# Products of the identity at the start of an attention and gated MLP kernel, and its last whole-tile store in two halves

## The chip, the cores and the metric

The kernel runs on one core of one Trainium2 chip. The metric is the device time of one execution in microseconds (us). Every time of the profile comes from one profiled execution, counted from its span's start.

## The reference

Batch 8, 16 query heads that share 4 key and value heads, 384 positions, head width 64. The attention's output, with its heads laid side by side, is the 1024-wide input x of a gated MLP:

```python
attn = softmax((q @ k.T) / sqrt(64))          # k, v repeated for 4 query heads each
x = (attn @ v).transpose(0, 2, 1, 3).reshape(8, 384, 1024)
h = maximum(x @ w_in, 0)                      # 1024 -> 1024
u, v = h[..., :512], h[..., 512:]
v_n = (v - mean(v)) / sqrt(var(v) + 1e-6)     # over the 512
v_s = einsum('ts,bsd->btd', w_spatial, v_n) + b_spatial[None, :, None]
out = (u * v_s) @ w_out                       # 512 -> 1024, float32
```

## The kernel before, in words

**Work of one batch.** Queries and keys are loaded as float32 (L199, L212), cast to 16 bits (L223, L234; the cast itself is in the helper `copy`, L322) and transposed, in batches 0 and 1 by TensorE against the identity (L328, L343, with a copy out of PSUM after it, L337, L352), from batch 2 on by transposing DMAs on SyncE's queue (L304, L313). A score step (`S`, L361) is two products of 64 rows that run side by side; its exponential (`E`, L375) is one ScalarE instruction of 128x1024. There are 18 of both in a batch, and two PSUM buffers for scores, so a score step waits for the exponential two before it. A value step (`X`, L386) is 12 products on 32-column parts, either of the values or of ones (the sums). The sums become reciprocals on ScalarE (`rl`, `re`; once on VectorE, `rv`), and `xm` (L418) multiplies into x transposed.

The MLP has the V products (`V` or, as halves of 64 rows, `v_part`), relu (`ru`), statistics (`bs`), `rs` and normalization (`nm`), the products with w_spatial (`SP`, `gs`) and their bias (`sa`), the U products (`U`, `gu`) and the gate (`gt`), and the output products (`O`, `go`) with their copies (`oc`) and stores (`st`, L560).

**Paired products.** A step `G` (L676) issues two chains of 64-row products that run side by side: the low rows of one tile with the high rows of another, in a first phase, and the rest in a second. The second phase must not start before the first has ended, and this is carried by a mark (`mk`, L689): a one-element memset on VectorE or GpSimd, which waits for the first phase in that engine's queue and on which the second phase waits. The kinds `w12`, `w24` and `w10` pair V products of one batch with output products of another.

**Weights.** w_in comes in 8 loads on GpSimd's queue (`lwi`, L245; part 1 is for V, part 0 for U). w_spatial comes in one load (`lws`), three GpSimd casts (`cws`, L269) and TensorE transposes (`Tw`), w_out in four loads (`lwo`, L252) that share two buffers, each cast in two halves (`cwo`). The transposing DMAs of batch 2 wait for all loads of w_in's part 0 (`behind_w_in`, L299).

**Order.** Three lists set the order: `FIRST` for batches 0 to 2 and what they prepare, `STEADY` for each of batches 3 to 6, and `LAST`. Each step names its kind, the batch (relative to the one run) and its arguments; the last letter of some names the engine (`p` GpSimd, `v` VectorE, `s` ScalarE). `run` (L727) goes through a list, and each engine, and each engine's DMA queue, executes its own steps strictly in the list's order. PSUM for all but the scores is four banks in a queue: `bank` takes the one free for longest, and the last reader gives it back, so the list also decides which reader a product waits for. A step `W` (L698) exists, but no list has it.

**The end.** The last output products are `O,0,2`, `O,0,3` and `lo,0,5` (L564). `lo` makes two pieces of 256 columns, one copied by VectorE and stored by SyncE, one copied and stored by ScalarE. `st,0,1` stores the tile of `O,0,2` and `O,0,3`, 128x1024.

Of the kernel before, what the change touches and what calls it, by code (L numbers as in the profile page):

```python
# [14 lines left out]
PE, POOL, SP = mybir.EngineType.PE, mybir.EngineType.Pool, mybir.EngineType.SP  # L15
# [3 lines left out]
SPLIT = 0  # L19

FIRST = """
lk,0,0,2 lq,0,0,0,1,0,1,s cq,0,0,0,1,1,0,1,s lq,0,1,0,1 cq,0,0,0,1,0,0,1,v lk,0,2,4 ck,0,0,0,3,p
Tq,0,0,0,0,1 Tk,0,0,0,3 tq,0,0,0,0,1,s lq,0,0,1,3 lq,0,1,1,3 tk,0,0,0,3,v lk,1 lv,0 ck,0,1,0,3,p S,0
S,0 lv,1 Tk,0,1,0,3 cq,0,1,0,1,0,0,1,p cq,0,1,0,1,1,0,1,p lq,1,0 lws,0 lq,1,1 Tq,0,1,0,0,1 lbi,0
lq,2,0 lq,2,1 lk,2 lwi,0,1,0 lwi,0,1,1 tk,0,1,0,3,v cq,0,0,1,3,1,0,1,p lwi,0,1,3 lwi,0,1,2
tq,0,1,0,0,1,v cq,0,0,1,3,0,0,1,v E,0 S,0 S,0 ck,1,0,0,3,p ck,1,1,0,3,p cv,0,p Tq,0,0,2,0,1 E,0 E,0
S,0 Tq,0,0,1,0,1 E,0 S,0 E,0 cq,0,1,1,3,1,0,1,v tq,0,0,1,0,1,v S,0 cq,0,1,1,3,0,0,1,v E,0
Tq,0,1,2,0,1 Tq,0,1,1,0,1 S,0 Tk,1,0,0,3 tq,0,1,1,0,1,v E,0 S,0 tk,1,0,0,3,v tq,0,0,2,0,1,v
tq,0,1,2,0,1,v E,0 X,0,0,2 rv,0,0 S,0 E,0 X,0,0,0 S,0 E,0 E,0 S,0 X,0,0,1 E,0 S,0 X,0,1,2 E,0
X,0,1,0 rl,0,1 cq,1,0,0,1,0,0,1,p lwi,0,0,2 cq,1,0,1,3,1,0,1,p xm,0,0,1 xm,0,0,0 S,0 S,0 cws,0,0  # L30
cws,0,1 lwi,0,0,3 cws,0,2 lwi,0,0,0 cq,1,1,0,1,0,0,1,p X,0,1,1 V,0,0,0,4 E,0 lwi,0,0,1 cv,1,p E,0
re,0,1 S,0 E,0 S,0 cq,1,1,1,3,0,0,1,p cq,1,0,0,1,1,0,1,s V,0,0,4,8 Tk,1,1,0,3 xm,0,1,1 xm,0,1,0
cq,2,0,0,3,1,0,1,p cq,2,0,0,3,0,0,1,p S,0 E,0 tk,1,1,0,3,v cq,1,0,1,3,0,0,1,v ru,0,0,v Tq,1,0,0,0,1
V,0,1,0,4 E,0 X,0,2,2 tq,1,0,0,0,1,s bs,0,0 rl,0,2 ck,2,1,0,3,p ck,2,0,0,3,p cq,2,1,0,3,0,0,1,p
X,0,2,1 S,0 S,0 cq,1,1,0,1,1,0,1,v re,0,2 E,0 X,0,2,0 cq,2,1,0,3,1,0,1,p Tq,1,1,0,0,1 xm,0,2,1
tq,1,1,0,0,1,v V,0,1,4,8 xm,0,2,0 S,0 S,0 ru,0,1,v E,0 Tq,1,0,1,0,1 Tw,0,2,3 Tq,1,0,2,0,1 V,0,2,0,4
cq,1,1,1,3,1,0,1,v S,0 S,0 E,0 tq,1,0,1,0,1,v tw,0,2,3 Tq,1,1,1,0,1 E,0 E,0 E,0 Tw,0,0,2 V,0,2,4,8
tq,1,1,1,0,1,v tq,1,0,2,0,1,v bs,0,1 tw,0,0,2 ru,0,2,s bs,0,2 X,1,0,2 rl,1,0 S,0 S,0 X,1,0,0 X,1,0,1
Tq,1,1,2,0,1 re,1,0 xm,1,0,0 S,0 E,0 xm,1,0,1 rs,0 E,0 nm,0,0 lwo,0,1 dq,2,0 nm,0,1 tq,1,1,2,0,1,v
nm,0,2 lwo,0,0 dk,2 dq,2,1 lwo,0,2 lwo,0,3 V,1,0,0,4 lv,2 V,1,0,4,8 E,0 S,0 G,0,gs,2,0,0,1 S,0  # L40
ru,1,0,v mk,0,gs,2,v G,0,gs,0,0,0,1 E,0 G,0,gs,2,1,0,1 S,0 mk,0,gs,0,v sa,0,2 G,0,gs,0,1,0,1 E,0 S,0
E,0 sa,0,3 sa,0,1 X,1,1,2 sa,0,0 E,0 rl,1,1 X,1,1,1 X,1,1,0 S,0 lq,3,1 lk,3 lq,3,0 re,1,1 E,0
G,0,gu,2,0,0 xm,1,1,1 xm,1,1,0 G,0,gu,2,0,1 S,0 S,0 G,0,gu,0,0,0 E,0 G,0,gu,0,0,1 S,0 mk,0,gu,2,v
cwo,0,0,0,v G,0,gu,2,1,0 cwo,0,1,0,p cwo,0,0,1,p mk,0,gu,0,p cwo,0,1,1,p S,0 G,0,gu,0,1,0 S,0
G,0,gu,0,1,1 E,0 gt,0,1 S,0 cwo,0,2,0,p E,0 G,0,gu,2,1,1 gt,0,2 gt,0,3 bs,1,0 gt,0,0 cwo,0,3,0,v E,0
cwo,0,2,1,p S,0 X,1,2,2 X,1,2,1 E,0 cwo,0,3,1,p S,0 S,0 V,1,1,0,4 E,0 V,1,1,4,8 E,0 rl,1,2 S,0
G,0,go,0,0,0 G,0,go,0,0,1 S,0 E,0 E,0 re,1,2 xm,1,2,1 mk,0,go,0,v E,0 G,0,go,0,1,0 E,0 S,0
G,0,go,0,1,1 S,0 cv,2,v ru,1,1,v oc,0,1,v oc,0,0,v cq,3,0,0,3,0,0,1,p cq,3,1,0,3,0,0,1,p E,0
cq,3,1,0,3,1,0,1,p cq,3,0,0,3,1,0,1,p X,1,2,0 xm,1,2,0 X,2,0,2 X,2,0,0 rl,2,0 E,0 S,0 E,0 re,2,0
G,1,w12,2,0,0 G,1,w12,2,0,1 S,0 S,0 bs,1,1 E,0 ck,3,0,0,3,v ck,3,1,0,3,v mk,1,w12,2,v G,1,w12,2,1,0  # L50
G,1,w12,2,1,1 E,0 S,0 S,0 oc,0,2,v ru,1,2,s oc,0,3,v xm,2,0,0 X,2,1,2 E,0 X,2,0,1 X,2,1,1 X,2,1,0
rl,2,1 bs,1,2 xm,2,0,1 re,2,1 S,0 xm,2,1,1 G,2,w24,0,0,0 G,2,w24,0,0,1 rs,1 S,0 E,0 S,0 E,0 E,0 lv,3
xm,2,1,0 mk,2,w24,0,v dk,3 dq,3,0 dq,3,1 nm,1,2 nm,1,0 nm,1,1 G,2,w24,0,1,0 oc,0,4,v G,2,w24,0,1,1
S,0 G,1,gs,0,0,0,1 E,0 ru,2,0,s oc,0,5,v mk,1,gs,0,v S,0 G,1,gs,0,1,0,1 E,0 G,1,gs,2,0,0,1 sa,1,1
mk,1,gs,2,v S,0 G,1,gs,2,1,0,1 sa,1,0 sa,1,2 sa,1,3 S,0 G,1,gu,0,0,0 G,1,gu,0,0,1 G,1,gu,2,0,0 S,0
mk,1,gu,0,v S,0 G,1,gu,2,0,1 G,1,gu,0,1,0 cv,3,p mk,1,gu,2,p S,0 G,1,gu,0,1,1 G,1,gu,2,1,0 E,0 E,0
E,0 S,0 G,1,gu,2,1,1 E,0 E,0 gt,1,0 gt,1,1 gt,1,3 gt,1,2 S,0 E,0 X,2,2,2 X,2,2,0 E,0 rl,2,2
G,2,w10,1,0,0 E,0 re,2,2 G,2,w10,1,0,1 S,0 S,0 E,0 mk,2,w10,1,v bs,2,0 xm,2,2,0 G,2,w10,1,1,0
G,2,w10,1,1,1 S,0 X,2,2,1 E,0 oc,1,1,s lk,4 st,0,0 lq,4,0 st,0,2 lq,4,1 ru,2,1,v xm,2,2,1 oc,1,0,v
st,0,1 E,0 bs,2,1 st,1,0 lv,4  # L60
"""

STEADY = """
X,0,0,2 cq,1,0,0,3,1,0,1,p cq,1,1,0,3,0,0,1,p cq,1,1,0,3,1,0,1,v X,0,0,0 rl,0,0 S,0 G,-1,w12,2,0,0
G,-1,w12,2,0,1 cq,1,0,0,3,0,0,1,p ck,1,1,0,3,p dq,1,1 re,0,0 E,0 ck,1,0,0,3,s S,0 mk,-1,w12,2,v dk,1
dq,1,0 S,0 G,-1,w12,2,1,0 G,-1,w12,2,1,1 E,0 xm,0,0,0 oc,-2,2,v X,0,1,2 E,0 ru,-1,2,s rl,0,1
oc,-2,3,s re,0,1 X,0,0,1 X,0,1,0 bs,-1,2 xm,0,0,1 X,0,1,1 S,0 xm,0,1,0 G,0,w24,0,0,0 G,0,w24,0,0,1
rs,-1 nm,-1,1 xm,0,1,1 mk,0,w24,0,v nm,-1,0 nm,-1,2 S,0 E,0 S,0 G,0,w24,0,1,0 oc,-2,4,v
G,0,w24,0,1,1 E,0 E,0 S,0 G,-1,gs,0,0,0,1 S,0 ru,0,0,s mk,-1,gs,0,p oc,-2,5,v E,0 G,-1,gs,2,0,0,1
bs,0,0 mk,-1,gs,2,v G,-1,gs,0,1,0,1 E,0 sa,-1,1 G,-1,gs,2,1,0,1 S,0 sa,-1,2 sa,-1,3 sa,-1,0 X,0,2,2  # L70
rl,0,2 X,0,2,0 X,0,2,1 S,0 G,-1,gu,0,0,0 G,-1,gu,0,0,1 S,0 re,0,2 E,0 E,0 xm,0,2,0 xm,0,2,1 E,0
G,-1,gu,2,0,0 G,-1,gu,2,0,1 S,0 mk,-1,gu,0,p E,0 G,-1,gu,0,1,0 G,-1,gu,0,1,1 S,0 E,0 mk,-1,gu,2,p
cv,1,p G,-1,gu,2,1,0 G,-1,gu,2,1,1 S,0 S,0 gt,-1,0 gt,-1,1 gt,-1,3 gt,-1,2 G,0,w10,1,0,0
G,0,w10,1,0,1 E,0 S,0 E,0 mk,0,w10,1,v S,0 G,0,w10,1,1,0 G,0,w10,1,1,1 oc,-1,0,v oc,-1,1,v ru,0,1,v
lq,2,0 lv,2 lk,2 S,0 lq,2,1 st,-2,2 st,-2,1 E,0 E,0 E,0 bs,0,1 st,-1,0
"""

LAST = """
S,0 X,0,0,2 E,0 G,-1,w12,2,0,0 G,-1,w12,2,0,1 S,0 mk,-1,w12,2,v S,0 E,0 rl,0,0 re,0,0 G,-1,w12,2,1,0
G,-1,w12,2,1,1 S,0 X,0,1,2 oc,-2,2,v X,0,0,1 oc,-2,3,v rl,0,1 re,0,1 E,0 ru,-1,2,v X,0,1,1 X,0,0,0  # L80
xm,0,0,1 xm,0,1,1 X,0,1,0 xm,0,0,0 S,0 G,0,w24,0,0,0 G,0,w24,0,0,1 E,0 mk,0,w24,0,v E,0 S,0 S,0 E,0
bs,-1,2 xm,0,1,0 G,0,w24,0,1,0 G,0,w24,0,1,1 E,0 oc,-2,4,v ru,0,0,s X,0,2,2 rl,0,2 re,0,2 rs,-1
oc,-2,5,s X,0,2,0 X,0,2,1 xm,0,2,0 xm,0,2,1 nm,-1,0 V,0,1,0,4 V,0,1,4,8 V,0,2,0,4 nm,-1,1 nm,-1,2
U,-1,1 V,0,2,4,8 ru,0,1,s SP,-1,0 SP,-1,1 bs,0,0 ru,0,2,v sa,-1,0 sa,-1,1 bs,0,2 gt,-1,1 bs,0,1
U,-1,0 SP,-1,2 SP,-1,3 rs,0 nm,0,1 sa,-1,2 sa,-1,3 nm,0,0 nm,0,2 gt,-1,0 U,0,0,1 U,-1,2 gt,-1,2
U,-1,3 SP,0,2 gt,-1,3 sa,0,2 SP,0,3 O,-1,4 U,0,2 SP,0,0 sa,0,3 sa,0,0 O,-1,2 O,-1,0 oc,-1,4,v gt,0,2
O,-1,1 oc,-1,0,s oc,-1,1,s O,-1,5 O,-1,3 SP,0,1 oc,-1,5,v oc,-1,2,v sa,0,1 U,0,1 U,0,3 gt,0,0 gt,0,1
gt,0,3 oc,-1,3,s st,-2,2 O,0,0,0,3 st,-2,1 st,-1,2 O,0,4 O,0,1,0,3 oc,0,4,s O,0,0,3,4 O,0,1,3,4
st,-1,1 st,-1,0 oc,0,1,v oc,0,0,s O,0,2 O,0,3 oc,0,2,s oc,0,3,s st,0,2,0,512 st,0,0 lo,0,5 st,0,1
"""  # L90


# [681 lines left out]
```

## Time and profile before

| | us |
|---|---|
| median of 7 runs (249.01 to 251.03) | 250.18 |
| the profiled execution | 249.8 |
| its span | 248.0 |
| TensorE busy, 2505 products | 237.1 |
| ScalarE busy, of it 140.3 in 144 exponentials | 187.4 |
| VectorE busy | 147.1 |
| GpSimd busy | 41.9 |
| DMA read, written | 25.95 MB, 12.58 MB |

A busy TensorE is counted from each product's start to its modelled end, so busy products overlap; the chain of waits, which follows the last instruction back to what released it, shows each product by the time it added. PE is TensorE, PEld its weight loads, DVE VectorE, ACT ScalarE, POOL GpSimd and SP SyncE; a q behind a name is that engine's queue. L366 is line 366 of the code.

### The profile page before, as it was taken

To read this page: it belongs to the slowest core of one execution; us is meant where nothing else is said; L and a number is where in the kernel's file an instruction comes from. 1 tells how busy PE (TensorE), PEld (TensorE's weight loads), DVE (VectorE), ACT (ScalarE), POOL (GpSimd) and SP (SyncE) were. 2 spreads that over 40 slices of the span, in tenths; PEclk is the share of its full clock that TensorE was granted. 3 is DMA by queue.
4 is the path that set the end of the run, shared out by engine and by line. 5 is a ranking of instruction groups with operands and counts; after the bars stand their busy time and mean duration, and the time that the engine had idled before them with its cause. 6 is when DMAs were issued, how large, how long until landed. Compare 5 with 4: busy or idle time off the path is not lost.

```text
span 248.0 us, 5946 instructions
## 1 busy us (share of the span) xinstructions
PE 237.1 (96%) x2505; PEld 112.7 (45%) x2505; DVE 147.1 (59%) x293; ACT 187.4 (76%) x242; POOL 41.9 (17%) x81
## 2 busy tenths in 40 slices
PE   1899999999999999999999999999999999999992
PEld 1334445544445444554455534554445544455451
DVE  0475867358763476835675377835676355678440
ACT  3899999998997797879987897879988777700222
POOL 1813824231401300020200130020300100000000
PEclk9999999999999999999999999999999999999998
DMA  8999999997699159229960689319844020030075
GB/s 177 288 230 347 222 244 282 181 303 225 83 266 340 47 166 179 94 60 355 202 185 3 196 310 178 116 48 281 256 86 172 3 85 3 27 146 0 0 292 216
DMA packets 57610, 42.71 MB, mean 172 GB/s; under 512 B 26864, under 2 KB 53872, under 8 KB 57584
## 3 DMA queue, kind: packets, MB, share of 16 engines
q1 hardware_dynamic: 54224, 39.85, 58.0%
q0 software_dynamic: 2176, 2.10, 5.5%
q10 hardware_dynamic: 1184, 0.39, 0.6%
q8 instruction: 19, 0.31, 0.5%
q14 instruction: 7, 0.06, 0.1%
HBM read 25.95 MB, written 12.58 MB: 155 GB/s over the span
## 4 chain that ended last, share of the span: by engine, by line
PE 90%; DMA 5%; ACT 1%; DVE 1%; issue 1%; SPq 0%; POOL 0%; DVEq 0%; POOLq 0%
PE X L393 20%; PE sc L366 14%; PE po L638 12%; PE pu L611 12%; PE pv L598 11%; PE pv L436 5%; DMA q<-in_q_dram 5%; PE psp L624 5%; PE po L543 4%; PE pu L508 4%; PE pq L347 2%; PE psp L482 2%; ACT aT L379 1%; PE sc_u L508 1%; DVE q L326 0%
## 5 line engine op out<-in xcount | busy, mean ns | idle before, releaser
L379 ACT ACTIVATE aT<-sc 128x1024 f16<-128x1024 f32 x144 | 140.3, 1022 | 20.9 <-PE sc L366 20.4
L638 PE MATMUL po<-w_out,gT 64*128 64x512 f16 x288 | 66.4, 376 | 0.1
L598 PE MATMUL pv<-w_in,xt 64*128 64x512 f16 x272 | 64.2, 376 | 0.0
L366 PE MATMUL sc<-qT,kT 64*128 64x512 f16 x288 | 51.9, 391 | 0.7 <-DVE kT L326 0.5
L422 DVE TENSOR_TENSOR xt<-X,rec 128x512 f16<-128x512 f32 x48 | 31.8, 683 | 12.3 <-ACT rec L410 5.4
L393 PE MATMUL X<-aT,v 128*32 128x512 f16 x576 | 36.3, 379 | 0.0
L611 PE MATMUL pu<-xt,w_in 64*128 64x384 f16 x384 | 35.5, 322 | 0.0
L638 PEld LDWEIGHTS <-gT 64*128 64x128 f16 x288 | 25.6, 94 | 17.0 <-DVE mark_v L692 4.2
L326 DVE COPY osb<-po 128x512 f32<-128x512 f32 x34 | 23.3, 690 | 16.6 <-PE po L638 11.0
L598 PEld LDWEIGHTS <-xt 64*128 64x128 f16 x272 | 25.2, 94 | 14.7 <-issue 0.8
L520 DVE SCALAR_TENSOR_TENSOR gT<-pu,v_s 128x384 f16<-128x384 f32 x31 | 16.0, 551 | 24.2 <-PE pu L611 23.2
L326 POOL CAST q<-q 128x768 f16<-128x768 f32 (+2 forms) x27 | 19.6, 747 | 46.3 <-DMA q<-in_q_dram 36.6
L366 PEld LDWEIGHTS <-kT 64*128 64x128 f16 x288 | 14.9, 94 | 25.4 <-issue 14.3
L611 PEld LDWEIGHTS <-w_in 64*128 64x128 f16 x384 | 18.7, 94 | 13.5
L393 PEld LDWEIGHTS <-v 128*32 128x32 f16 x576 | 16.1, 96 | 14.9 <-issue 2.4
L494 DVE TENSOR_TENSOR v_s<-psp,bias_b 128x384 f32<-128x384 f32 x32 | 20.1, 681 | 4.0 <-PE psp L624 2.6
L457 DVE BATCH_NORM_STATS2 stats<-v_r 128x6 f32<-128x512 f32 x24 | 16.6, 691 | 7.9 <-ACT v_r L449 3.2
L393 PE MATMUL X<-aT,ones 128*32 128x512 f16 x288 | 20.2, 382 | 0.2
L404 ACT ACTIVATE rec<-X 128x512 f32<-128x512 f32 x23 | 13.8, 601 | 7.7 <-PE X L393 7.5
L324 ACT ACTIVATE osb<-po 128x512 f32<-128x512 f32 x13 | 7.7, 594 | 14.7 <-PE po L543 14.7
L694 POOL MEMSET mark_p<- 1x1 f32 x14 | 1.2, 88 | 86.7 <-PE pu L611 43.8
L410 ACT ACTIVATE rec<-rec 128x512 f32<-128x512 f32 x23 | 14.5, 631 | 0.5
(55 smaller groups left out, 187.5 us busy)
## 6 DMA issues: line engine op xcount, KB each, us to landing
out_dram<-osb SPq DMA_DIRECT2D x23, 512.0 KB, 5.0
q<-in_q_dram SPq DMA_DIRECT2D x14, 768.0 KB, 8.0
v<-in_v_dram SPq DMA_DIRECT2D x8, 384.0 KB, 4.5
k<-in_k_dram SPq DMA_DIRECT2D x7, 384.0 KB, 4.4
w_in<-in_moe_w_in_dram POOLq DMA_DIRECT2D x8, 256.0 KB, 7.0
w<-in_moe_w_out_dram SPq DMA_DIRECT2D x4, 512.0 KB, 5.5
q<-in_q_dram SPq DMA_DIRECT2D x2, 512.0 KB, 6.6
ws<-in_moe_w_spatial_dram SPq DMA_DIRECT2D x1, 576.0 KB, 9.5
```

Source lines behind the costliest of these rows:

```text
L326: engine.tensor_copy(dst, src)
L366: nc.tensor.matmul(sc[:, half, 0 : 512 // js], kT[b][lo:hi, gp, t, :], qT[b, gp][lo:hi, qt, j0::js], start=True, stop=True,)
L379: nc.scalar.activation(aT[b, qt][:, gp, t].rearrange("p h (j q) -> p h j q", j=G)[:, :, j0::js], held["sc", b, u, j0][:, :, 0 : 512 // js] ...
L393: nc.tensor.matmul(dst[32 * g : 32 * (g + 1), :], v16[:, g, t, 32 * part : 32 * (part + 1)] if part < 2 else ones32, a[:, g // 2, t, g % 2 ...
L410: nc.scalar.activation(r, r, AF.Exp, scale=-1.0)
L422: nc.vector.tensor_tensor(xt[:, jj, :, qt * P : (qt + 1) * P], held["X", b, qt, jj].rearrange("p (j q) -> p j q", j=G), held["rec", b, qt] ...
L457: nc.vector.bn_stats(s6, held["v_r", b, st])
L494: nc.vector.tensor_tensor(held["v_s", b][:, m, :].rearrange("p (t s) -> p t s", t=NST), held["psp", b, m][:, 0:S].rearrange("p (t s) -> p ...
L520: nc.vector.scalar_tensor_tensor(held["gT", b][:, mu, :], held["pu", b, mu][:, 0:S], 0.0, held["v_s", b][:, mu, :], op0=ALU.max, op1=ALU.mult,
L598: yield lambda kc=kc: nc.tensor.matmul(held["pv", b, st], xT[b][rows, kc, st * P : (st + 1) * P], w_in16[rows, kc, DH:DFF], start=(first a ...
L611: yield lambda kc=kc: nc.tensor.matmul(held["pu", b, mu][:, 0:S], w_in16[rows, kc, mu * P : (mu + 1) * P], xT[b][rows, kc, :], start=(firs ...
L638: yield lambda m=m: nc.tensor.matmul(held["po", b, i], held["gT", b][rows, m, tt * P : (tt + 1) * P], w_out16[rows, m, half * 512 : (half ...
```

## The change

All of it is in the three lists. The functions are the same; the lines of the code move by 2.

- `FIRST` has 19 steps `W` with 51 products of the identity by itself, each 128x128 into a bank of PSUM: 33 ahead of the first transposes, the others among the first score steps.
- The order of `FIRST`, `STEADY` and `LAST` is new throughout, and some steps are on other engines. The useful steps are the same ones.
- In `LAST`, `st,0,1` becomes two stores of 512 columns, ahead of `lo,0,5`.

The first lines of `FIRST`:

```diff
-lk,0,0,2 lq,0,0,0,1,0,1,s cq,0,0,0,1,1,0,1,s lq,0,1,0,1 cq,0,0,0,1,0,0,1,v lk,0,2,4 ck,0,0,0,3,p
-Tq,0,0,0,0,1 Tk,0,0,0,3 tq,0,0,0,0,1,s lq,0,0,1,3 lq,0,1,1,3 tk,0,0,0,3,v lk,1 lv,0 ck,0,1,0,3,p S,0
-S,0 lv,1 Tk,0,1,0,3 cq,0,1,0,1,0,0,1,p cq,0,1,0,1,1,0,1,p lq,1,0 lws,0 lq,1,1 Tq,0,1,0,0,1 lbi,0
-lq,2,0 lq,2,1 lk,2 lwi,0,1,0 lwi,0,1,1 tk,0,1,0,3,v cq,0,0,1,3,1,0,1,p lwi,0,1,3 lwi,0,1,2
...
+lk,0,0,2 W,0,2 W,0,4 W,0,2 W,0,4 lq,0,0,0,1,0,1,s cq,0,0,0,1,1,0,1,p W,0,4 W,0,4 W,0,2 W,0,4 W,0,4
+ck,0,0,0,3,s W,0,2 W,0,1 lq,0,1,0,1 cq,0,0,0,1,0,0,1,v Tk,0,0,0,3 Tq,0,0,0,0,1 lk,0,2,4
+tq,0,0,0,0,1,v lq,0,0,1,3 tk,0,0,0,3,s lq,0,1,1,3 ck,0,1,0,3,p lk,1 lv,0 cq,0,1,0,1,1,0,1,p
+cq,0,1,0,1,0,0,1,p lwi,0,1,2 lwi,0,1,1 lv,1 lwi,0,1,3 W,0,3 W,0,2 cq,0,1,1,3,1,0,1,p S,0 W,0,4 S,0
+W,0,1 lq,1,0 Tk,0,1,0,3 Tq,0,1,0,0,1 S,0 W,0,1 E,0 lq,1,1 E,0 tk,0,1,0,3,v tq,0,1,0,0,1,v S,0 lws,0
+lk,2 W,0,2 lwi,0,1,0 ck,1,0,0,3,p ck,1,1,0,3,p cv,0,p S,0 W,0,4 cq,0,0,1,3,0,0,1,v
+cq,0,0,1,3,1,0,1,v lbi,0 lq,2,0 Tq,0,0,1,0,1 S,0 Tq,0,0,2,0,1 cq,1,0,0,1,0,0,1,p cq,0,1,1,3,0,0,1,v
+tq,0,0,1,0,1,v S,0 Tq,0,1,1,0,1 W,0,1 Tq,0,1,2,0,1 E,0 lq,2,1 S,0 Tk,1,0,0,3 E,0 tq,0,0,2,0,1,v E,0
...
```

The order of the weights' loads and casts in the rest of `FIRST`, by queue (the other steps of these queues left out where "..." stands):

```
SyncE before:   lq,1,0 lws,0 lq,1,1 lbi,0 lq,2,0 lq,2,1 lk,2 lwo,0,1 dq,2,0 lwo,0,0 dk,2 dq,2,1 lwo,0,2 lwo,0,3
SyncE after:    lq,1,0 lq,1,1 lws,0 lk,2 lbi,0 lq,2,0 lq,2,1 dk,2 lwo,0,0 dq,2,0 lwo,0,1 dq,2,1 lwo,0,2 lwo,0,3
GpSimd before:  cq,1,0,0,1,0 lwi,0,0,2 cq,1,0,1,3,1 cws,0,0 cws,0,1 lwi,0,0,3 cws,0,2 lwi,0,0,0 cq,1,1,0,1,0 lwi,0,0,1 cv,1
GpSimd after:   cq,1,0,0,1,0 lwi,0,0,0 cq,1,1,0,1,0 lwi,0,0,3 cq,1,0,1,3,0 cq,1,0,1,3,1 cws,0,0 lwi,0,0,1 cq,1,1,1,3,1 cws,0,2 cws,0,1 lwi,0,0,2
GpSimd, w_out:  before cwo,0,1,0 cwo,0,0,1 mk,0,gu,0 cwo,0,1,1 cwo,0,2,0 cwo,0,2,1 cwo,0,3,1
                after  cwo,0,0,0 mk,0,gu,2 mk,0,gu,0 cwo,0,1,0 cwo,0,3,1 mk,0,go,0
VectorE after:  ... xm,1,1,1 xm,1,1,0 cwo,0,0,1 cwo,0,1,1 gt,0,0 gt,0,3 gt,0,2 cwo,0,2,1 gt,0,1 cwo,0,2,0 ru,1,1 ...
ScalarE after:  ... rl,1,2 E,0 E,0 cwo,0,3,0 re,1,2 ...
```

`STEADY`:

```diff
-X,0,0,2 cq,1,0,0,3,1,0,1,p cq,1,1,0,3,0,0,1,p cq,1,1,0,3,1,0,1,v X,0,0,0 rl,0,0 S,0 G,-1,w12,2,0,0
-G,-1,w12,2,0,1 cq,1,0,0,3,0,0,1,p ck,1,1,0,3,p dq,1,1 re,0,0 E,0 ck,1,0,0,3,s S,0 mk,-1,w12,2,v dk,1
-dq,1,0 S,0 G,-1,w12,2,1,0 G,-1,w12,2,1,1 E,0 xm,0,0,0 oc,-2,2,v X,0,1,2 E,0 ru,-1,2,s rl,0,1
...
-G,0,w24,0,1,1 E,0 E,0 S,0 G,-1,gs,0,0,0,1 S,0 ru,0,0,s mk,-1,gs,0,p oc,-2,5,v E,0 G,-1,gs,2,0,0,1
-bs,0,0 mk,-1,gs,2,v G,-1,gs,0,1,0,1 E,0 sa,-1,1 G,-1,gs,2,1,0,1 S,0 sa,-1,2 sa,-1,3 sa,-1,0 X,0,2,2
...
-G,0,w10,1,0,1 E,0 S,0 E,0 mk,0,w10,1,v S,0 G,0,w10,1,1,0 G,0,w10,1,1,1 oc,-1,0,v oc,-1,1,v ru,0,1,v
-lq,2,0 lv,2 lk,2 S,0 lq,2,1 st,-2,2 st,-2,1 E,0 E,0 E,0 bs,0,1 st,-1,0
+ck,1,0,0,3,p ck,1,1,0,3,p X,0,0,2 rl,0,0 X,0,0,0 S,0 G,-1,w12,2,0,0 G,-1,w12,2,0,1 re,0,0 S,0 S,0
+E,0 E,0 cv,1,p cq,1,0,0,3,1,0,1,p cq,1,1,0,3,1,0,1,p cq,1,0,0,3,0,0,1,p xm,0,0,0 mk,-1,w12,2,v
+cq,1,1,0,3,0,0,1,s G,-1,w12,2,1,0 G,-1,w12,2,1,1 oc,-2,3,s dq,1,0 oc,-2,2,s dk,1 S,0 lv,2 st,-2,1
+dq,1,1 lk,2 ru,-1,2,v X,0,1,2 lq,2,1 lq,2,0 X,0,0,1 X,0,1,0 X,0,1,1 bs,-1,2 xm,0,0,1 rl,0,1 re,0,1
...
+S,0 E,0 G,0,w24,0,1,0 E,0 oc,-2,4,v G,0,w24,0,1,1 S,0 G,-1,gs,0,0,0,1 mk,-1,gs,0,p ru,0,0,s
+oc,-2,5,v S,0 G,-1,gs,2,0,0,1 G,-1,gs,0,1,0,1 mk,-1,gs,2,p E,0 S,0 G,-1,gs,2,1,0,1 sa,-1,0 sa,-1,1
...
+G,0,w10,1,0,1 E,0 S,0 S,0 E,0 E,0 mk,0,w10,1,v E,0 G,0,w10,1,1,0
+G,0,w10,1,1,1 S,0 ru,0,1,s oc,-1,0,v oc,-1,1,v st,-1,0 st,-2,2 bs,0,1 E,0
```

The end of `LAST`:

```diff
...
-gt,0,3 oc,-1,3,s st,-2,2 O,0,0,0,3 st,-2,1 st,-1,2 O,0,4 O,0,1,0,3 oc,0,4,s O,0,0,3,4 O,0,1,3,4
-st,-1,1 st,-1,0 oc,0,1,v oc,0,0,s O,0,2 O,0,3 oc,0,2,s oc,0,3,s st,0,2,0,512 st,0,0 lo,0,5 st,0,1
...
+gt,0,1 sa,0,3 O,-1,2 st,-1,2 U,0,3 gt,0,3 oc,-1,2,s O,0,1,0,3 O,0,4 O,0,1,3,4 O,0,0,0,3 oc,0,4,s
+st,-1,0 st,-1,1 O,0,0,3,4 O,0,2 O,0,3 st,0,2,0,512 oc,0,0,v oc,0,1,s oc,0,2,v oc,0,3,s st,0,0
+st,0,1,0,512 st,0,1,512,1024 lo,0,5
```

## The prediction

> **What bounds the kernel now.** I read the page's busy table and its chain by engine first, then the chain in order of time, the instruction groups kept apart by shape, and for each disputed step the instructions of one engine in order of time.
>
> The busy table and the chain by engine, from the page:
>
> ```profile
> PE 237.1 (96%) x2505; PEld 112.7 (45%) x2505; DVE 147.1 (59%) x293; ACT 187.4 (76%) x242; POOL 41.9 (17%) x81
> PE 90%; DMA 5%; ACT 1%; DVE 1%; issue 1%; SPq 0%; POOL 0%; DVEq 0%; POOLq 0%
> ```
>
> TensorE is the chain. So a gain can come only from three places: the start, before TensorE has enough to do; places inside where it waits; and the tail after its last product. The start, from the chain in order of time (start, length, what):
>
> ```profile
> 0.78 3.97 DMA q<-in_q_dram
> ...
> 5.24 0.61 PE pq L347 x4
> ...
> 6.62 0.63 PE sc L366 x2
> ...
> 7.27 1.95 ACT aT L379 x2
> ...
> 12.71 0.98 PE pq L347 x8
> 13.70 0.54 PE sc L366 x2
> 14.24 0.43 PE pk L332 x3
> 14.67 0.33 PE sc L366 x2
> 14.99 0.76 PE X L393 x12
> ```
>
> Q lands at 4.75, TensorE first works at 5.24, ScalarE's first exponential starts at 7.27. The same score product takes 0.54 to 0.63 until 13.70 and 0.33 from 14.67. The groups by shape say it per instruction: 614 ns from 5 to 9 us and 382 ns from 20 to 30 us, and 311 ns against 222 ns for a transpose. So TensorE runs slowly for its first 9 us although the page's clock row shows 9 throughout. From 14.67 to 243.41 the chain is TensorE nearly without a hole. One of the few holes, in the chain of a steady batch:
>
> ```profile
> 137.88 8.45 DMA q<-in_q_dram
> ...
> 146.42 0.95 DVE q L326
> ...
> 147.46 0.39 PE po L638
> ```
>
> A cast of q stands at the head of VectorE's queue and waits for its load; the mark queued behind it is late, and a product that costs 0.21 in its neighbours costs 0.39. The tail, SyncE's queue in order of time:
>
> ```profile
> 235.77 6.20 SPq L562 DMA_DIRECT2D out_dram<-osb  x4
> 243.44 0.33 SPq L584 DMA_DIRECT2D out_dram<-osb  x1
> 243.87 0.38 SPq L562 DMA_DIRECT2D out_dram<-osb  x1
> ```
>
> The last whole-tile store goes behind the last piece, at 243.87. In 0.2 us slices, its transfers stop from 243.8 to 244.2, then run at about 370 GB/s until 246.4; the span ends at 248.0.
>
> **Part 1, the identity products.** There are 51, of 128x128, on the identity that GpSimd finishes at 1.31. Four cold transposes take 0.61 in the chain with a latency of 0.31, so one costs (0.61-0.31)/3 = 0.10. The 33 ahead of the first transposes run from 1.35 to about 4.7, beside the loads: K's transpose can start at about 4.2 (load 3.69, a ScalarE cast of about 0.5) and Q's at 5.2 as before, so they cost at most 0.5 on K and nothing on Q. The other 18 (5 ahead of the first score, 4 and 1 around the second, 8 among the next scores) cost 1.8 cold or, at the 0.055 of a warm transpose in the chain, 1.0; they lie where TensorE waits for copies or exponentials (0.97 apiece in ScalarE's row of seven in 6.77). Without that cover the 5 around the second score delay K's second transpose by 0.3 to 0.5.
>
> What is gained depends on when the clock rises. The row: from the first product at 5.24 it took 9 us of patchy work. By that, products from 1.35 bring the rise to about 10.5. The Trainium skill ("TensorE: Matmul & The Clock Gate", Part 1) says that the array is at half rate until one window of about 3.4 us, which runs freely and isn't reset by the kernel, was busy throughout. By that the rise comes between 4.8 and 8.2. The page also speaks against the change: it puts the loss to the ramp under 1% of a kernel, and says (Part 4) that transposes don't count as busy, so only what the 51 do counts. No run here shows the window's phase.
>
> By the row: the first score can start at 6.32, because the copies of the first transposes change engines (VectorE's 0.42 for Q in place of ScalarE's 0.60), but the delay on K's second transpose eats that at the third exponential (9.28 against 9.2). What remains is the hole of 0.24 that ScalarE shows at 14.28: gain 0.2. By the rule at its early end: Q's transpose and the score take about 0.5 less, the first exponential starts at 6.55, the ninth score at 13.4 against 14.67. TensorE gains 1.3, but ScalarE is full from 7.27 to 34 (24 exponentials at 0.97 and 3.5 of other work are 26.8 of 26.7), so only its own 0.72 + 0.24 = 0.96 comes through. I take 0.7, nearer to the rule, because the 33 leave no hole. Ends: -0.3 to 1.1.
>
> **Part 2, the new order of the first batches.** The list is rewritten throughout; the useful products, and, to one, the changes between 64-row, 32-column and full-array products (a switch costs about 0.1), stay the same in number. Two steps lose slack. The load of w_spatial goes behind Q's second half, so its casts start at about 28 in place of 24.26, with a w_in issue and a Q cast between them: the transposes of w_spatial are ready at 31 to 31.5, where TensorE arrives at about 31. Cost 0 to 0.6; I take 0.1. The K transpose of batch 2 waits for the last w_in load (issued at 27.98 before, about 31.2 after, 8.5 from there to the transpose's release as before: 39.7), and two loads of w_out are now behind it. W_out's fourth load then lands at about 55.4 (first 40.2 + 5.7, casts, second 43.1 + 6.5, casts, fourth 50.0 + 5.4); its casts end at 56.0, and TensorE needs them at about 55.9. Cost 0 to 0.5; I take 0.1.
>
> **Part 3, the steady batches.** One period of TensorE is 28.29, 28.05, 28.31 and 28.25 by the starts of the same product at 64.71, 93.00, 121.05, 149.36 and 177.61. 28.05 is the period without a hole. The list now issues the next Q loads in mid-batch, ahead of two stores, and puts the casts on GpSimd and ScalarE, so no mark stands behind a load on VectorE; the marks of the spatial products go to GpSimd as well. That frees 0.24 + 0.26 + 0.20 = 0.7. ScalarE takes 0.9 more per batch (23.4 to 24.3 of 28), and its relu at the batch's end frees a bank 0.2 ahead of the product that needs it. Cost 0 to 0.1 a batch; net gain 0.5, ends -0.4 and 0.8.
>
> **Part 4, the last batch and the store.** TensorE has no hole there before, so the new order can only lose. Walking its banks from 212.8 with the durations of the rows, the tightest is the relu before the third V product (ready 217.6, needed 217.67). Cost 0 to 0.4, taken as 0.1. The store's first half needs a VectorE copy of 0.69 from 241.69, goes at 242.4, the second at 243.2 after ScalarE's copy; SyncE issues the last piece about 0.1 later, which nothing waits for, since ScalarE's piece goes at 243.84 anyway. The same 768 KB then start as the previous store's data ends, 243.8 in place of 244.2: 0.4. Ends 0.1 and 0.7; the lower one because the second issue and its landing (2.0 for 256 KB) may end last.
>
> **Sum.** 0.7 - 0.1 - 0.1 + 0.5 - 0.1 + 0.4 = 1.3. The profiled execution took 249.8 with a span of 248.0, so its like is 248.5; the median of the runs is 250.18, 0.4 above it, and I predict for it: 248.9.
>
> **Rivals.** *All of it works* (12%): the clock rises at 5, nothing new waits: 1.0 + 0.7 + 0.6 = 2.3, so 247.9. *The clock doesn't rise in time or ScalarE keeps the pace* (20%): the products do nothing for the end. For it: ScalarE's full row, and the patchy 9 us. Against it: the ninth score is late by TensorE's own cold transposes (12.71 to 14.67). Time: 250.18 - 0.2 (hole) - 0.3 (marks) - 0.4 + 0.3 = 249.6. *The last weights come late* (22%): the K transpose that blocks SyncE for w_in delays w_out, and VectorE and ScalarE have a w_out cast in mid-queue, with gates and exponentials behind it. One w_out load took 9.2 rather than 5.5 (the one issued at 31.91). If the second load does so, it lands at 52.3, the fourth at 58.4, the casts end at 59.0: 3.1 of waiting less the 1.3 of the sum is 1.8 slower: 252.0. It decides once the fourth load lands after about 56.8 (1.3 of wait cancels the sum). Against it: before, three of four took 5.3 to 5.7.
>
> **Numbers.** A measurement of this kernel can tell about 0.3%, 0.75 us. The likeliest case (46%, 248.0 to 249.4) and all-of-it are faster: 58%. The clock rival is within: 20%. Late weights are slower: 22%. The range, 247.6 to 251.3, leaves out about half of that last case and the low end of the second.
>
> **What would show it.** Right: score products near 380 ns by 8 us, a first exponential near 6.7, an X product at 14.2, four periods near 28.05 and no query cast ahead of a mark, last data about 246.0 less the shift. Wrong: 600 ns scores beyond 9 us; TensorE waiting for a w_out cast near 55 or a w_spatial cast near 31; ScalarE or VectorE idle before a cast on a DMA; periods over 28.3; a first exponential no earlier than 7.2.

## The result, and the profile after

The changed kernel's median is 248.34 us (14 runs, 247.57 to 249.02). The kernel before, run beside it on the same chip, has 249.80 (35 runs, 249.01 to 251.61). The ratio is 0.9935, with a 95% interval of 0.9918 to 0.9952, so the kernel is faster by about 1.6 us, give or take 0.4. The forecast was 1.3 faster. The profiled execution of the changed kernel took 248.88 with a span of 247.1, against 249.8 and 248.0 before: 0.9 less. It lies near the upper end of the changed kernel's times, about half a microsecond above their median.

The page's busy table and its chain by engine, changed kernel:

```profile
PE 239.1 (97%) x2556; PEld 120.4 (49%) x2556; DVE 143.0 (58%) x280; ACT 190.6 (77%) x249; POOL 43.0 (17%) x87
...
PE 84%; ACT 10%; DVE 3%; issue 1%; POOL 0%; POOLq 0%
```

TensorE was 90% of the chain and is 84%; ScalarE was 1% and is 10%. Some of that is the start, where the chain now ran through nine exponentials in a row. The rest is a new thing: places up to 73 us where TensorE waits for ScalarE and VectorE. The start, chain in order of time (start, length, what):

```profile
1.37 3.70 PE warm L705 x33
5.07 0.32 PE pk L334 x3
5.39 0.51 PE pq L349 x4
5.89 0.53 PE warm L705 x5
6.43 0.61 PE sc L368 x2
7.03 0.02 issue
7.05 8.36 ACT aT L381 x9
15.42 0.04 issue
15.46 0.39 PE sc L368 x2
```

The 33 products took until 5.07. TensorE is no longer what the start waits for: nine exponentials stand end to end, where before TensorE's slow transposes and scores held up the ninth score. When the clock rose is read from TensorE in order of time, whose lines are start, length, instruction:

```profile
5.28 0.61 PE L349 MATMUL pq<-ident,q 128*128 128x128 f16 x4
...
6.41 0.61 PE L368 MATMUL sc<-qT,kT 64*128 64x512 f16 x2
6.95 0.49 PE L705 MATMUL warm<-ident 128*128 128x128 f16 x4
7.37 0.39 PE L368 MATMUL sc<-qT,kT 64*128 64x512 f16 x2
...
13.95 0.83 PE L395 MATMUL X<-aT,ones 128*32 128x512 f16 x12
```

The same score step takes 0.61 at 6.41 and 0.39 at 7.37, so in this execution the rise fell at about 7. The first value product starts at 13.95; before, it was 14.93 in this view.

The tail, SyncE's queue in order of time. The four stores in the first line include both halves of the last tile, and only the last piece's store comes behind them:

```profile
239.96 3.14 SPq L564 DMA_DIRECT2D out_dram<-osb  x4
243.19 0.41 SPq L586 DMA_DIRECT2D out_dram<-osb  x1
```

The row of DMA activity from 242 to 247, in slices of 0.125 us, is `9799989999799999999899989994` and zeros after it; before it was `0005699998999700006995899979979999910000`. The hole from 243.8 to 244.2 is gone and the data ends at about 245.5, not 246.4. From the start of ScalarE's last copy to the end of the span it is 4.1 us (242.96 to 247.1), before 4.6 (243.43 to 248.0).

Last, one place that costs. The chain where the second batch's normalization meets the paired products of the group `w24`:

```profile
66.17 0.91 ACT aT L381
67.08 0.19 ACT rstd L464
...
67.30 0.21 ACT rstd L465
...
67.53 1.03 DVE v_n L470
68.56 0.60 DVE xt L424
69.16 0.49 DVE v_n L470 x2
69.65 0.05 issue
69.70 0.39 PE po L640
```

An output product at 69.70 costs 0.39, its neighbours 0.21, and what released it is VectorE's mark behind that chain. The list of waits of weight loads for marks has the size of it: of its three numbers (sum, count, longest in us) the last is 0.9, and it was 0.6.

```profile
PEld L640 <- DVE mark_v L694: 3.0, 10, 0.9
```

Before, the chain in the same place goes through two score steps between the phases, and TensorE has no hole:

```profile
69.24 0.21 PE pv L598
...
69.46 0.43 PE sc L366 x4
69.89 0.21 PE po L638
```

The new list puts one score step there (0.22). In sum these waits are smaller than before (`PEld L638 <- DVE mark_v L692: 4.2, 14, 0.6`); it is the longest one that grew.

### The profile page after: what moved, and what is told of

It reads as the page before. It is cut to its first block, busy times and chain, and to the rows that moved or that the text cites. A ratio compares the mean times of both kernels' runs of the same rounds, so it can differ in the third digit from the quotient of the medians.

```text
span 247.1 us, 6053 instructions
## 1 busy us (share of the span) xinstructions
PE 239.1 (97%) x2556; PEld 120.4 (49%) x2556; DVE 143.0 (58%) x280; ACT 190.6 (77%) x249; POOL 43.0 (17%) x87
## 4 chain that ended last, share of the span: by engine, by line
PE 84%; ACT 10%; DVE 3%; issue 1%; POOL 0%; POOLq 0%
PE X L395 18%; PE pu L613 13%; PE sc L368 11%; PE po L640 11%; PE pv L600 11%; ACT aT L381 7%; PE psp L626 4%; PE po L545 4%; PE pv L438 4%; PE pu L510 4%; PE warm L705 2%; PE psp L484 2%; DVE v_n L470 1%; DVE v_s L496 1%; ACT rec L412 1%; ACT rec L406 1%
## 5 line engine op out<-in xcount | busy, mean ns | idle before, releaser
L381 ACT ACTIVATE aT<-sc 128x1024 f16<-128x1024 f32 x144 | 139.8, 1025 | 17.3 <-PE sc L368 17.2
L368 PE MATMUL sc<-qT,kT 64*128 64x512 f16 x288 | 50.5, 380 | 1.3 <-ACT aT L381 1.3
L328 DVE COPY osb<-po 128x512 f32<-128x512 f32 x28 | 19.3, 690 | 15.4 <-PE po L640 9.2
L368 PEld LDWEIGHTS <-kT 64*128 64x128 f16 x288 | 15.9, 94 | 23.1 <-issue 11.9
L613 PEld LDWEIGHTS <-w_in 64*128 64x128 f16 x384 | 20.5, 94 | 11.9
L328 POOL CAST q<-q 128x768 f16<-128x768 f32 (+2 forms) x29 | 21.2, 754 | 24.8 <-DMA q<-in_q_dram 17.2
L326 ACT ACTIVATE osb<-po 128x512 f32<-128x512 f32 x19 | 10.6, 595 | 18.1 <-PE po L545 17.4
L696 POOL MEMSET mark_p<- 1x1 f32 x19 | 1.9, 100 | 104.7 <-PE psp L626 70.8
L449 DVE TENSOR_SCALAR v_r<-pv 128x512 f32<-128x512 f32 x12 | 8.2, 687 | 13.2 <-PE pv L600 10.7
```

Of the source, the lines that this page charges most:

```text
L328: engine.tensor_copy(dst, src)
L368: nc.tensor.matmul(sc[:, half, 0 : 512 // js], kT[b][lo:hi, gp, t, :], qT[b, gp][lo:hi, qt, j0::js], start=True, stop=True,)
L381: nc.scalar.activation(aT[b, qt][:, gp, t].rearrange("p h (j q) -> p h j q", j=G)[:, :, j0::js], held["sc", b, u, j0][:, :, 0 : 512 // js] ...
L613: yield lambda kc=kc: nc.tensor.matmul(held["pu", b, mu][:, 0:S], w_in16[rows, kc, mu * P : (mu + 1) * P], xT[b][rows, kc, :], start=(firs ...
```

## The experiments

Each ratio is against the kernel before, run beside it on the same chip; 1 us is 0.004 of it. Where a trace is read, it is of one execution.

**No products.** The changed kernel without its 19 steps `W`; nothing else is removed, and the products of the identity are no part of the output.

```diff
-W,0,2 W,0,4 W,0,2 W,0,4 ... W,0,1
```

> The changed kernel without its 51 identity products; all else, the new order and the split store too, as changed. Theory A (the products bring the clock up early, but the later waits on ScalarE's chain near 36, 52 and 70 us give most of it back): the ninth score and the first X product come about 1 us later than in the changed kernel (X at 14.9 against 13.95), score products stay at 600 ns until past 10 us, and the end is 0.3 to 0.7 us later than the changed kernel's, so 0.9 to 1.3 us below the kernel before. Rival B (ScalarE alone sets the end of the first batches, so the products are worth nothing): the same 1.6 us below the kernel before as the changed kernel. Rival C (the products are the whole gain): no faster than the kernel before.

249.53 (249.01 to 250.02): 0.9982 [0.9968, 0.9995], 0.45 faster than before, and not the 0.9 to 1.3 that was expected. Against the changed kernel's 0.9935, the products are worth 1.2 us (0.6 to 1.7, the two intervals taken as independent). TensorE in order of time, without the products:

```profile
9.03 0.61 PE L365 MATMUL sc<-qT,kT 64*128 64x512 f16 x2 [0.16 <-ACT aT L378]
9.99 0.61 PE L365 MATMUL sc<-qT,kT 64*128 64x512 f16 x2 [0.34 <-ACT aT L378]
...
14.63 0.61 PE L365 MATMUL sc<-qT,kT 64*128 64x512 f16 x2
15.17 1.18 PE L392 MATMUL X<-aT,ones 128*32 128x512 f16 x12
```

Scores stay at 0.61 until past 14.63, and the first value product starts at 15.17, 1.22 later than with the products. Its first exponential, at 7.04, is as early as the changed kernel's in the profiled execution (7.05): the gain was made behind it, in the scores that no longer fall behind. Of those 1.22, 0.79 are left at the stall of the figure above (70.49 without products, 69.70 with) and 0.8 in the span (247.9 and 247.1). The stall itself is of one size in both, so it does not eat the products' gain. Where the rest of the lead went is told below.

**Products alone.** The kernel before, with 51 products at the same places among its own steps: 33 ahead of the first transposes, 18 among the first scores.

```diff
-Tq,0,0,0,0,1 Tk,0,0,0,3
+W,0,4 W,0,4 W,0,4 W,0,4 W,0,4 W,0,4 W,0,4 W,0,4 W,0,1 Tq,0,0,0,0,1 Tk,0,0,0,3
-S,0
+W,0,3 W,0,2 S,0 W,0,4
...
```

> The kernel before with 51 identity products put into its first list at the same places (33 ahead of the first transposes, 18 among the first scores), nothing else changed. Theory A: 382 ns scores from about 7 us, the first X product at about 14.0 in place of 14.93, and as the old order of the first batches shows no wait on ScalarE in its chain after 15 us, more of that comes through: 0.5 to 0.9 us faster. Rival B: no change within 0.2 us. Rival C: 1.6 us faster.

249.19 (248.56 to 250.01): 0.9967 [0.9954, 0.9981], 0.8 faster. TensorE in order of time:

```profile
5.22 0.40 PE L347 MATMUL pq<-ident,q 128*128 128x128 f16 x4 [0.41 <-ACT q L324]
...
13.77 0.83 PE L393 MATMUL X<-aT,ones 128*32 128x512 f16 x12
```

The rise came before 5.22, and the first value product 1.16 earlier than before. At the next tile's value product the lead is 0.49 (33.40 against 33.89). What took the rest stands between, on TensorE and on ScalarE (in brackets the idle time before, and what ended it):

```profile
27.93 0.40 PE L347 MATMUL pq<-ident,q 128*128 128x128 f16 x4 [0.60 <-POOL q L326]
29.56 1.94 ACT L379 ACTIVATE aT<-sc 128x1024 f16<-128x1024 f32 x2 [1.05 <-PE sc L366]
```

TensorE waits for a cast of q on GpSimd, and ScalarE, far from full, waits for TensorE. The chain runs from that cast back through GpSimd's queue to a load of q that landed at 22.26. Load and queue do not come earlier because TensorE does, so this wait keeps part of the lead. Whether the new list keeps more of it than the old one (1.2 against 0.8) is inside the intervals of the medians; the traces, compared below, say yes.

**The 33 alone and the 18 alone.** Both are the changed kernel with the other products left out.

```diff
-W,0,3 W,0,2 ... S,0 W,0,4 S,0 W,0,1 ... (the 18; second kernel: the 33)
```

> The changed kernel with only the 33 identity products ahead of the first transposes; the 18 among the first scores left out. Theory D ([...]with all 51 the rise came at 4.2 to 6.9 us in the five profiles so far): the 33 and the transposes keep TensorE busy from 1.37 to about 5.9, which holds a whole window only in some executions, so the kernel lies between the changed one and the one without products: 0.7 to 1.4 us faster than the kernel before, with a wider spread of its times. Rival (the 33 do it all): 1.6 us, like the changed kernel.

> The changed kernel with only the 18 identity products among the first scores; the 33 left out. Theory D: TensorE starts at 5.2 and the rise comes after one busy window, at 9 to 12 us in place of 14 to 16: 0.6 to 1.1 us faster than the kernel before (without any products 0.45). Rival (the 18 only take time): 0.45 us or less.

With the 33: 248.73, 0.9945 [0.9917, 0.9973]. Its ten times fall in two groups, 247.8 to 248.2 and 249.3 to 250.1, five in each, with nothing between. With the 18: 249.71, 0.9997 [0.9970, 1.0024], and wide, 248.46 to 251.57. The profiled execution with the 33 is of the early group (247.95): its first transposes are already short, 0.33 for three at 4.79 (0.50 without products). With the 18 (profiled: 248.64) a score takes 0.61 at 9.78 and 0.39 at 10.74. So the 33 can do all of it, but not in every execution, and the kernel lies inside its expectation. Why the later group is later was not profiled. A later rise of the clock could do it, and so could either of two other losses that single executions show below, of about 0.5 and 0.9; the 14 times of the changed kernel, with both sets, have no such group. The 18 missed their expectation of 0.6 to 1.1. Their profiled execution, the second fastest of its kernel, shows the rise between 9.78 and 10.74, where it was expected, but in the median no gain over the kernel before can be told.

**The split store alone, and the reverse.** The kernel before with the new stores; then the changed kernel with the old one.

```diff
-st,0,0 lo,0,5 st,0,1
+st,0,0 st,0,1,0,512 st,0,1,512,1024 lo,0,5
```

> The kernel before with only the last whole-tile store in two halves ahead of the last pieces. Theory A: the end of TensorE's work stays (243.4), the last data ends 0.4 us earlier because the transfers follow the previous store without the gap of 0.4: 0.4 us faster. Rival: the last small store's landing sets the end and the two halves delay it: 0 to 0.1 us faster, or slower.

> The changed kernel with its last whole-tile store whole again and behind the last pieces. Theory: 0.45 us slower than the changed kernel, so 1.2 us faster than the kernel before; the last data ends 3.0 us after TensorE's last product in place of 2.5. Rival (the order of the last batch, not the split, frees the store): the same as the changed kernel.

Alone: 249.57, 0.9982 [0.9965, 0.9999], 0.45 faster. The reverse: 249.13, 0.9966 [0.9946, 0.9986], that is 0.8 slower than the changed kernel (0.1 to 1.4). The traces say 0.45 both ways at the tail. SyncE's queue, changed kernel with the old store:

```profile
243.21 0.33 SPq L585 DMA_DIRECT2D out_dram<-osb  x1
243.64 0.38 SPq L563 DMA_DIRECT2D out_dram<-osb  x1
```

The last store is again issued last, 0.45 behind the changed kernel's last one. From the start of ScalarE's last copy to the end it is 4.6 us, as before. Only this tail is compared: the profiled execution, with 249.55 the slowest of its kernel, lost 0.9 in another place (see the first list below).

**The steady list alone.** The kernel before with the new `STEADY`, and the same again with a load of v moved ahead.

```diff
-oc,1,1,s lk,4 ... st,1,0 lv,4
+oc,1,1,s lv,4 lk,4 ... st,1,0
```

> The kernel before with only the new order of the steady batches. Theory A (the query cast ahead of a mark in VectorE's queue costs 0.2 to 0.26 us in most batches): the periods of TensorE are 28.05 to 28.1 and the whole is 0.4 to 0.7 us faster. Rival (a hole filled there opens elsewhere, since ScalarE has 0.9 us more to do a batch): within 0.2 us of the kernel before, periods near 28.2.

> As the run with only the new steady order, but batch 4's V load, which the old first list issues last of all (behind a store that waits to 88 us) and which the new steady list's casts on GpSimd now stand behind, is moved ahead of batch 4's K load at the end of the first list. Theory (the new steady order is good for 0.35 us, and the mixed kernel lost 0.8 once, near 100 us, because the cast of V waits for its late load and the K transpose behind it came late): the wait near 100 us goes and the kernel is 0.2 to 0.6 us faster than the kernel before. Rival (the steady order itself is worth nothing or costs): still slower or the same.

Without the move: 250.45, 1.0023 [1.0008, 1.0038], 0.6 slower, where 0.4 to 0.7 faster was expected. With it: 249.58, 0.9981 [0.9958, 1.0005], which is unclear, 0.5 faster at the middle. The waits of the slower one between 86 and 104 us:

```profile
POOL v L326 <- DMA v<-in_v_dram: 14.1, 1, 14.1
...
PEld L366 <- DMA kT<-k: 1.1, 1, 1.1
```

The old first list issues this v behind a store that waits until 89.2, and the steady list's work behind it loses about 0.9 once, near 100 us (10.34 between two value products that are 9.43 apart before). This is an artefact of joining two lists, not a property of the change. With v early it is gone, and the value product of each batch comes at 102.26, 130.34, 158.42 and 186.50: three periods of 28.08.

**The last list alone.** The kernel before with the new `LAST`, its store left whole and last.

> The kernel before with only the new order of the last batch, the last whole-tile store left whole and behind the last pieces. Theory D: the small waits of 0.06 to 0.16 us that the old last batch shows between 214 and 236 us go: TensorE's last products from the first X of its third query tile on take 29.4 us in place of 29.75, 0.2 to 0.4 us faster. Rival (as the prediction had it, no hole to fill): within 0.1 us.

249.86, 1.0004 [0.9980, 1.0027]: no difference that the runs can tell, and so not the 0.2 to 0.4 that was expected. In its trace the stretch from the last batch's first V product to the last output products is 27.35 us, against 27.65 before.

**All parts on the old first list.** The old `FIRST` with the 51 products and v early, the new `STEADY` and `LAST`, the split store. The diff is the sum of those above.

> The old order of the first batches with the 51 products and the early V load, the new steady batches, the new last batch and the split store. Theory D (what the runs so far say: the products are worth 0.8 to 1.2 and most comes through, the new order of the first batches costs about 1.0 in waits between 36 and 72 us, the steady order gives 0.35, the last batch 0.25, the split store 0.45): 1.9 to 2.4 us faster than the kernel before, and faster than the changed kernel (1.6). Rival (the new first batches are needed for the others' gains): no more than 1.6 us.

248.19 (247.74 to 249.84): 0.9929 [0.9901, 0.9956], 1.8 faster than before. This kernel has every part of the change but the rest of the new first list. If that rest cost what the trace without products suggests, about 0.9, this one would be ahead of the changed kernel by as much; 1.9 to 2.4 was expected. It is ahead by 0.15 at the middle, give or take 0.8, so a cost of that size is at the edge of what the runs allow.

**The stall at the mark.** First the mark is moved from VectorE to GpSimd; then the statistics of two batches are also moved ahead of an exponential, and a normalization ahead of a copy.

```diff
-mk,2,w24,0,v
+mk,2,w24,0,p
```

```diff
-S,0 E,0 xm,1,0,1 rs,0
+S,0 rs,0 E,0 xm,1,0,1
-nm,0,1 tq,1,1,2,0,1,v ... nm,0,0
+nm,0,1 nm,0,0 tq,1,1,2,0,1,v
-xm,2,1,1 E,0 rs,1
+xm,2,1,1 rs,1 E,0
```

> The changed kernel with one mark of the first list (batch 2's w24 group) on GpSimd in place of VectorE, where it stands behind two normalizations that wait for ScalarE. Theory: the second phase of that group no longer starts at 69.7 but near 69.1, and 0.4 to 0.6 us of the whole goes (2.0 to 2.2 below the kernel before). Rival (the wait moves on to the spatial products, which need the same normalizations near 71.8): within 0.2 us of the changed kernel.

> The changed kernel with that mark on GpSimd, the two small ScalarE instructions that make 1/sqrt of the variance of batches 0 and 1 each moved ahead of one exponential, and batch 0's third normalization ahead of a copy on VectorE. Theory: both waits of the chain through ScalarE (near 36 to 39 and 66 to 70 us) shrink, 0.8 to 1.2 us faster than the changed kernel (2.4 to 2.8 below the kernel before). Rival (ScalarE keeps the pace, an exponential later is a score later): 0 to 0.4 us faster than the changed kernel.

The mark alone: 248.55, 0.9928 [0.9901, 0.9956]. The mended order: 248.21, 0.9926 [0.9895, 0.9957]. Neither can be told from the changed kernel, nor from each other, so both missed their expectations (2.0 to 2.2 and 2.4 to 2.8 below the kernel before). The traces tell more. From the third batch's value step of its second tile to the w_spatial products that follow, it is 7.03 us before, 7.62 in the changed kernel, 7.60 with the mark moved and 7.27 mended. The chain with the mark moved:

```profile
67.91 0.02 PE po L639
67.94 0.02 issue
67.96 0.02 POOLq L695
67.98 0.07 issue
68.05 0.44 POOL mark_p L695
68.49 0.05 issue
68.53 0.39 PE po L639
```

The mark now has nothing ahead of it in its queue, and between the end of the first phase (67.93) and the second (68.53) there is still 0.6, of which a score covers 0.2 and TensorE idles 0.40. With the mark on VectorE it idled 0.42, so moving it gained nothing here: what is left is the mark's own way there and back, and it has too little work beside it. In the mended kernel the memset takes 0.10 and the product follows 0.27 after the first phase. The memset took 0.44 while VectorE ran two normalizations (67.45 to 68.45), and 0.10 while VectorE was idle; whether that is the cause was not tried.

## Why the prediction was right, and where its terms were off

**Sign and size.** Predicted 1.3 faster (248.9 from 250.18); measured 1.6. (The 250.18 is a median of 7 runs; the 35 beside the changed kernel have 249.80.) Each term beside what the runs gave (minus is slower):

| term | predicted | by medians | by traces |
|---|---|---|---|
| identity products | 0.7 | 1.2 (0.6 to 1.7) | 0.8 |
| new first list | -0.2 | open: 0 to -1 | -0.9 without products, 0 to -0.5 with |
| steady list | 0.5 | 0.5 (-0.1 to 1.0) | 0.35 |
| last list | -0.1 | none told | 0.3 |
| split store | 0.4 | 0.45 and 0.8 | 0.45 |
| sum | 1.3 | 1.6 (the kernel itself) | 1.0 |

The traces' terms add up to 1.0, against 0.9 between the two spans; these are of single executions, each with its own moment of the clock's rise. The 1.6 of the medians is the answer for the kernel. That 1.3 came so near is in part luck: the products were under-sized, the first list's cost has other causes than the two it was put down to, and the last list's sign was wrong, though by too little for the medians to tell. The products and the first list also do not simply add, as shown next.

**Products: the mechanism held, the size was low, and the cap was not the one forecast.** The clock rose early, near the rule that the Trainium skill states ("TensorE: Matmul & The Clock Gate", Part 1: a free-running window of about 3.4 us), which gave 4.8 to 8.2, and not at 10.5 as the row of before would have it. With all 51 products, the first transposes of the short duration begin at 4.5 to 5.4 in five traces (in two of them the rise lies before 4.7, a little ahead of what the rule gave); in the profiled changed kernel it fell at about 7. That execution has a first exponential at 7.05, against the 6.7 of the forecast; five others with all 51, in the old or the new list, have 6.43 to 6.76. The forecast took 0.7 as the middle of early and late rises; with all 51 the early rise is the usual one.

The forecast let at most 0.96 through, because ScalarE's row was full from 7.27 to 34. It was not: before, it has idle time of 0.24 at 14.28, 0.38 at 30.05 and 0.18 at 32.17. What became of the lead can be read from three places in the profiled executions (start of batch 0's first value product, of batch 2's, and the span):

| kernel | first | batch 2 | span |
|---|---|---|---|
| before | 14.93 | 64.64 | 248.0 |
| old list, products alone | 13.77 | 64.14 | 247.3 |
| new list, no products | 15.17 | 64.88 | 247.9 |
| changed (new list, late rise) | 13.95 | 64.03 | 247.1 |
| new list, mark on GpSimd (early rise) | 13.37 | 62.88 | 245.9 |
| new list, the 33 alone (early rise) | 13.54 | 63.06 | 246.1 |

In the old list a lead of 1.16 shrinks to 0.50, by the wait for the load and cast of q shown above. In the new list with an early rise the whole of it arrives, more than the 0.96: 1.80 and 1.63 at first, 2.00 and 1.82 at batch 2, 2.0 and 1.8 in the span, all against the kernel without products. In the changed kernel's trace 0.8 of 1.22 arrives, and here the loss stands between two value products of batch 0:

```profile
36.48 1.51 DVE L470 TENSOR_SCALAR v_n<-v_r,mv,rstd 128x512 f16<-128x512 f32 x2
39.01 0.66 PE L626 MATMUL psp<-wsT,v_n 64*128 64x384 f16 x6 [0.39 <-DVE v_n L470]
```

The two normalizations run while GpSimd casts a q (from 36.63, 2.05 long). They take 1.51, and 1.00 to 1.01 in the seven traces where GpSimd is idle beside them; TensorE waits for them, and from 32.97 to 41.71 it takes 8.74 where four other traces of the new list take 8.18. So the late rise (0.3 to 0.6) and this meeting (about 0.5) are both in the execution that lies half a microsecond above its median; that they are the cause of that was not tried.

**First list: two small costs forecast, neither as forecast.** The forecast put 0.1 on late w_spatial casts and 0.1 on late w_out weights. In the changed kernel's trace neither came. The casts of w_spatial began at 27.1 (28 forecast) and TensorE found them ready. W_out's fourth load landed at 52.7 (55.4 forecast), its last cast ended at 55.3, and the output products went at 54.63 without a wait for it. The last w_in load was issued at 30.2, not 31.2, and the transposing DMA behind it went at 38.0, not 39.7.

The rival of late weights is real all the same. The kernel with the old store has the same first list, and in its profiled execution the chain runs through the second and the fourth load of w_out, and a cast on ScalarE with exponentials behind it:

```profile
44.44 5.51 DMA w<-in_moe_w_out_dram
...
50.90 4.31 DMA w<-in_moe_w_out_dram
55.21 0.02 issue
55.23 0.63 ACT w_out L325
```

The fourth load landed at 55.21, as forecast, and from 41.20 to 58.58 this execution took 17.38, where all others take 16.48: 0.9 lost. No load was a slow one, so it was not the 3.1 of waiting that the rival had; how often the smaller loss comes is not known.

What the list costs elsewhere depends on the products. Without them it stands behind the kernel before by 0.24 at the first value product, 0.5 at the first w_spatial products (40.04 against 39.54), and 1.0 at the next batch's (72.61, with one score step of 0.22 fewer done, against 71.83). The last half microsecond is the stall at the mark. Against it stands one stall that the old list has and the new one hasn't, 0.56 at 73.25, where a mark waits behind an addition on VectorE. By the traces the first list then costs 0.9 of the span. With products and an early rise it costs nothing against the old list with products, which keeps part of their lead back as shown: from the first value product to batch 3's it takes 78.79 and 78.77 (mark on GpSimd, the 33 alone), and 78.83 with all parts on the old list. The changed kernel itself, with the meeting on VectorE, takes 79.36. This fits the medians, where all parts on the old list are only 0.15 ahead of the changed kernel; they allow a cost between nothing and 1 us.

**Steady list.** Predicted four periods near 28.05: three are 28.09, 28.09 and 28.08 by the starts of one product from 93.38 on, against 28.05, 28.31 and 28.25 before. The first, which still runs mostly in the first list, is 29.28 (64.03 to 93.31) against 28.29, so the 0.24 that the forecast counted there did not come. The hole at a query's cast is gone from the chain, and GpSimd's casts of q wait for their loads 17.2 us in all, against 36.6. The 0.03 a batch above the forecast period is in place of the 0 to 0.1 that was allowed for.

**Last batch.** The step "TensorE has no hole there before, so the new order can only lose" was wrong in the trace: of two like w_spatial steps in the chain of before the second costs 0.16 more.

```profile
226.94 0.49 PE psp L482 x3
...
227.44 0.65 PE psp L482 x3
```

The new list has no such hole, and the stretch is 0.3 shorter in both traces that have it; the rest of the 0.3 is not accounted for. It is too little for the runs to tell.

**Store.** Forecast: data starts at 243.8 in place of 244.2 and ends 0.4 earlier. This is what the trace has, 0.45. The medians of the two kernels that isolate it give 0.45 and 0.8; between them the runs cannot choose.

## What to carry to other kernels

A start where TensorE runs in patches can stay slow for 9 us (a transpose 311 ns, and 222 later), and the page's clock row does not show it: compare the length of one kind of product early and late. Idle TensorE time ahead of the first load can be filled with products that nobody reads. What that returns is decided by the next wait that does not move with TensorE: in the old list a load and a cast behind it kept half of the lead, in the new list all of it could arrive. When an order is rewritten for one purpose, walk each mark between two phases: here it took 0.27 to 0.6 us there and back, two score steps (0.43) covered it and one (0.22) did not. A wait that is absent from one execution can stand in another, as the late weights did.

## What the runs showed of the hardware

The clock's rise differs between executions of like kernels. With 51 products from 1.37 on, the 33 ahead of the transposes took 3.29, 3.30 and 3.70 in three traces, and the first transposes afterwards were short (0.40 for four, 0.33 for three) in the first two and not in the third (0.53 for three). In the first of these all 33 were done by 4.66. At the 0.112 apiece of the third trace they would have needed 3.70, so the rise lies inside them, less than 3.3 us after the first product started. A window of about 3.4 us that had to be busy from end to end, as the Trainium skill has it ("TensorE: Matmul & The Clock Gate", Part 1), would have begun before the products did. The measurement decides: either the window is shorter, or not all of it need be filled, and the runs do not say which. They do show that a transpose's length follows the clock (311 and 222 ns); whether transposes count towards its rise none shows.

The first two of three normalizations on VectorE took 1.51 together beside GpSimd's casts, against 1.01 where GpSimd stood idle; the third took 0.71 and, in another trace beside a cast, 0.96, against 0.53. A memset of one element on GpSimd, used as a mark, took 0.44 beside two normalizations and 0.10 beside an idle VectorE. All this was seen and not tried apart.
